# One fused attention and expert kernel: low parts of late weights on VectorE, low hidden products last, the last pair of heads two slots later

## The chip, the cores and the metric

The kernel runs on one core of one Trainium2 chip. The metric is the device time of one execution in microseconds. TensorE (PE in the profile) multiplies matrices, VectorE (DVE), ScalarE (ACT) and GpSimd (POOL) work elementwise, and SyncE (SP) and ScalarE issue the transfers. Each engine works through its own queue in order. "Idle" in a row is the time for which an engine stood still just before an instruction, with what ended it.

## The reference, cut to what matters

```python
# attention: 2 x 8 heads, 576 positions, head size 64
scores = scale * np.matmul(q, k.transpose(0, 1, 3, 2))
kth = np.partition(scores, -32, axis=-1)[..., -32:-31]
scores = np.where(scores >= kth, scores, -1e9)
attn = exp(scores - max); attn /= attn.sum(-1) + 1e-9
x = attn @ v                       # as 1152 tokens x 512
# part 1: 4 experts, 1024 hidden
p = domain_probs / domain_probs.sum(-1)
out = sum(p[:, e] * (np.maximum(x @ w1[e], 0) @ w2[e]) for e in range(4))
# part 2: 768 hidden, weights in float64
h = np.maximum(np.maximum(out @ m1, out @ m2), out @ m3)
return h @ mo
```

The weights of the first part are float32. Those of the second come as float64 and are converted on the chip.

## The kernel before, in words

The 1152 tokens are nine tiles of 128. Attention goes through 36 pairs (tile, two heads), eight slots each. `attention()` puts every step of a pair into a slot by a preset (`LOOSE`, `TIGHT` and so on, with the slots of `pv`, `turn`, `rec`, `last`), and yields once per slot.

Matrix products in float32 are made of three fast ones: each operand is split into a high part (rounded) and a low part (the rest). `product()`, lines 677 to 683, issues three matmuls: high times low, high times high, low times high. A weight of 128x1024 is loaded by SyncE, its high part `whi` is copied by ScalarE (L272), and its low part `wlo` is a subtraction on GpSimd (in two halves) or VectorE (whole), both at L278. `W_AHEAD` = 4 weights are split ahead of use. A weight's place in the list, counted from the first of stage 7, is `late`: below zero it goes to GpSimd, from there on by turns to GpSimd (even) and VectorE (odd).

Part 1 runs in stages over one to three tiles. Stage 0 is tile 0 alone and has its own code (`first_alone`). Stages 1 to 6 have two tiles, stage 7 has three (tiles 6, 7, 8) and stage 8 two (7, 8). Each stage does half of the experts' hidden blocks: for each i of four, `half1` for two units (first layer, ReLU on ScalarE, low part by a subtraction that reads PSUM on VectorE, L825, or, each fourth time, on GpSimd through a copy in SBUF, L816 to L818), and then `half2` of the i before (second layer, accumulated over an even and an odd i in one PSUM bank per tile). After an odd i the sum is scaled by the gate into `acc` (L742, L744).

`experts()` and the later stages are one generator of TensorE work. The main loop keeps two planned times, of TensorE and of VectorE, and after each slot lets out products until TensorE's planned time reaches the goal, which grows with VectorE's. Evacuations are queued by `later()`, and each `tick()` issues the next step of all that are queued.

From slot 306 on, one piece of the second part's weights per two slots goes through `to_float32`: two steps on ScalarE, three on VectorE (L242, L244, L246), an integer add on GpSimd (L249), and a store issued by ScalarE (L254) three slots later. Once attention has run out of slots, each slot adds `PAUSE` = 0.8 us to the goal.

Behind stage 8, `turned()` transposes three `acc` tiles into `x2`, high part on ScalarE (L907), low part `x2l` on VectorE (L908), for `largest()`, the second part. Its weights go by turns to GpSimd and VectorE too.

Of the kernel before, what the change touches and what calls it, by code (L numbers as in the profile page):

```python
# [10 lines left out]
F32 = mybir.dt.float32  # L11
# [49 lines left out]
def kernel(  # L61
# [41 lines left out]
    HALVES = [range(E) if not n % 2 else range(E, 2 * E) for n in range(len(STAGES))]  # L103
    WHOLE = [n for n, x in enumerate(STAGES) if len(x) == 1]
    FIRST_IN = {t: min(n for n, x in enumerate(STAGES) if t in x) for t in range(NTILE)}
# [93 lines left out]

    def whole(key):  # L200
        return key[1] in "ab" and key[0] in WHOLE

    def w_load_to(n):
        while w_pos["load"] < min(n, len(order)):
            key, src = order[w_pos["load"]]
            if key[1] in "cd" and narrowed[0] < WIDE * (narrow_at[key[2:]] + 1):
                return
            if whole(key):
                w_pos["load"] += 1
                continue  # L210
            raw = wp.tile([P, 1024], F32, tag="raw", bufs=5, name="raw")
            nc.sync.dma_start(out=raw, in_=src)
            w_raw[key] = raw
            w_pos["load"] += 1
# [42 lines left out]
    def w_split_to(n):  # L257
        while w_pos["split"] < min(n, len(order)):
            w_load_to(w_pos["split"] + 1)
            if w_pos["load"] == w_pos["split"]:  # L260
                return
            key, src = order[w_pos["split"]]
            if whole(key):
                w_hl[key] = wp.tile([P, 1024], F32, tag=("hi", "lo")[key[3]], name="whole")
                nc.sync.dma_start(out=w_hl[key], in_=src)
                w_pos["split"] += 1
                w_load_to(w_pos["split"] + 3)
                continue
            raw = w_raw.pop(key)
            hi = wp.tile([P, 1024], F32R, tag="hi", name="whi")  # L270
            lo = wp.tile([P, 1024], F32R, tag="lo", name="wlo")
            nc.scalar.activation(out=hi, in_=raw, func=AF.Copy)  # L272

            late = w_pos["split"] - w_index[LATE, "a", HALVES[LATE][0], 0]
            on = nc.vector if late >= 0 and late % 2 else nc.gpsimd

            for x in (slice(0, 512), slice(512, 1024)) if on is nc.gpsimd else (slice(0, 1024),):
                on.tensor_tensor(out=lo[:, x], in0=raw[:, x], in1=hi[:, x].bitcast(F32), op=ALU.subtract)  # L278
            f = 512 if key[1] in "bd" else 256
            w_hl[key] = (hi.rearrange("p (a f) -> p a f", f=f), lo.rearrange("p (a f) -> p a f", f=f))  # L280
            w_pos["split"] += 1
            w_load_to(w_pos["split"] + 3)

    def weight(key, oldest=None):

        w_split_to(w_index[oldest or key] + W_AHEAD + 2 * whole(key))
        return w_hl[key]
# [270 lines left out]
    def attention():  # L558
# [4 lines left out]

        def options(n):
            return TIGHT if n == HP - 1 else SECOND if n == 2 * HP - 1 else MIDDLE if n in (HP - 2, 2 * HP - 3, 2 * HP - 2) else FIRST if n < 2 * HP else THIRD if n == 3 * HP - 1 else BOTH if n in ON_ACT[1] else LOOSE

# [30 lines left out]
        for n, (c, hp, t) in enumerate(pairs):  # L597
# [25 lines left out]
            two(s0 + o.get("turn", o["rec"] + 2), pr.trans_r)  # L623
            end = max(o["pv"], o["rec"] + 2) + o["lag"]
            if "norm" in o:
# [164 lines left out]
    def experts():  # L790
        begin = {}

        def half1(c, i, u):
            tiles = STAGES[c]
            N = len(tiles) * P
            if c in WHOLE:
                ps = bank("ps1")
                w = weight((c, "a", i, u)).rearrange("p (a f) -> p a f", f=256)
                for f in range(2):
                    for a in range(KT):  # L800
                        pe(4 * P)
                        nc.tensor.matmul(ps[:, f * P:(f + 1) * P], lhsT=w[:, a, f * P:(f + 1) * P], rhs=xfull[:, a, :], start=f == a == 0, stop=f == 1 and a == KT - 1)
                    yield True
                h = hp_.tile([P, 2, 512], F32, tag="h", bufs=4, name="hfull")[:, 0, 0:2 * P]
                later(lambda: [nc.scalar.activation(out=h, in_=ps[:, 0:2 * P], func=AF.Relu), made.add(("h", c, i, u))])
                yield h
                return
            for groups in layer1(weight((c, "a", i, u)), xs_of(tiles), N, begin.pop((c, i, u), None)):
# [4 lines left out]
            count = made_h[0] = made_h[0] + 1  # L813
            if ON_POOL_H and not count % ON_POOL_H:
                raw = ms.tile([P, 2 * WIDTH], F32, tag="tm", bufs=2, name="raw")
# [15 lines left out]

        def half2(c, i, hs, ti):
            t = STAGES[c][ti]
            if not i % 2:
                outs[t] = po.tile([P, DM], F32, tag="o", name="ps2") if ti < 2 else bank("ps2")
            ps = outs[t]
            assert {("h", c, i, 0), ("h", c, i, 1)} <= made
            if c in WHOLE:
                for u in range(2):
                    w = weight((c, "b", i, u), (c, "b", i, 0)).rearrange("p (f n) -> p f n", f=2)  # L840
                    for f in range(2):
                        pe(4 * DM)
                        nc.tensor.matmul(ps, lhsT=hs[u][:, f * P:(f + 1) * P], rhs=w[:, f, :], start=not i % 2 and u == f == 0, stop=i % 2 == 1 and u == f == 1)
                        yield True
            else:
                yield from layer2(ps, [weight((c, "b", i, u), (c, "b", i, 0)) for u in range(2)], hs, len(STAGES[c]) * P, ti, not i % 2, i % 2 == 1)
            if not i % 2:
                return
            first = t not in accs
            if first:  # L850
                sums(t)
            later(*[lambda: None] * E_LAG, gated(ps, t, i // 2, first, c == LAST_IN[t] and i == HALVES[c][-1]))

        before = None
        for c in range(1, len(STAGES)):
# [14 lines left out]
            for i in HALVES[c]:  # L870
                hs = []
                for u in range(2):
                    for y in half1(c, i, u):
                        if y is not True:
                            hs.append(y)
                        yield True
                if i == HALVES[c][-1]:
                    x_free.update(t for t in STAGES[c] if LAST_IN[t] == c)
                if before is not None:
                    for ti in range(len(STAGES[before[0]])):  # L880
                        yield from half2(*before, ti)
                before = c, i, hs
        flush()
        yield from turned_ahead(len(STAGES))
        for ti in range(len(STAGES[before[0]])):
            yield from half2(*before, ti)
        flush()
# [193 lines left out]
```

## Time and profile before

| | |
|---|---|
| median of 3 runs | 752.12 us (752.11 to 752.51) |
| profiled execution, time | 752.02 us |
| profiled execution, span | 750.2 us |
| TensorE busy with matmuls | 721.8 us, 96% |
| mean granted TensorE clock | 0.997 |

The span runs from the first to the last instruction. The time of the profiled execution holds 1.8 us more than its span. A matmul's busy time overlaps the next one's, so the starts of two successive matmuls tell the rate.

### The profile page before, as it was taken

The page shows a single profiled execution, that of the slowest core. Times are in us where ns is not written, and L with a number is a line of the kernel's source. Part 1 is how long each engine was busy: PE and PEld are TensorE (multiplying, and loading weights), DVE is VectorE, ACT ScalarE, POOL GpSimd, SP SyncE. Part 2 cuts the span into 40 slices and gives each one's busy share as a digit, 9 for nine tenths or more (in the row PEclk, how much of TensorE's full clock was granted, in tenths as well). Part 3 has the DMA queues.
Part 4 walks back from the last instruction along what each step waited for, and adds up shares of the span by engine and source line. Part 5 has one row for each costly group of instructions (what it writes and reads, how often), then busy time and mean ns, then how long its engine had stood idle before and what let it go on. Part 6 is the DMA issues. An engine that isn't in the chain of part 4 may idle for free. (4 is left out here: it accounts for less than half of the span.)

```text
span 750.2 us, 13770 instructions
## 1 busy us (share of the span) xinstructions
PE 721.8 (96%) x4758; PEld 642.7 (86%) x4758; DVE 579.1 (77%) x1161; ACT 508.0 (68%) x1137; POOL 495.2 (66%) x432
## 2 busy tenths in 40 slices
PE   6799999999999999999999998999999899999998
PEld 3576788888989989898989977899989799999996
DVE  6999989989999899999999964887778544233341
ACT  4668889899978787788788856576656633433531
POOL 2514778679979797697778659888768743442520
PEclk9999999999999999999999999999999999999999
DMA  7584565535647364445444355889979742453501
GB/s 221 179 267 158 154 183 159 154 127 159 192 123 212 110 189 124 149 134 166 134 132 153 114 183 168 298 297 301 297 239 314 257 149 82 151 172 99 195 4 42
DMA packets 56487, 130.16 MB, mean 173 GB/s; under 512 B 9761, under 2 KB 23329, under 8 KB 56417
## 3 DMA queue, kind: packets, MB, share of 16 engines
q1 hardware_dynamic: 48064, 120.69, 51.5%
q10 hardware_dynamic: 8352, 8.59, 3.2%
q8 instruction: 37, 0.61, 0.3%
q14 instruction: 34, 0.27, 0.1%
HBM read 120.60 MB, written 8.65 MB: 172 GB/s over the span
## 5 line engine op out<-in xcount | busy, mean ns | idle before, releaser
L278 POOL TENSOR_TENSOR wlo<-raw,whi 128x512 fp32r<-128x512 f32 x258 | 340.4, 1348 | 119.4 <-ACT whi L272 115.9
L272 ACT ACTIVATE whi<-raw 128x1024 fp32r<-128x1024 f32 x164 | 169.7, 1056 | 36.2 <-PE ps L683 12.9
L681 PE MATMUL ps<-xl,whi 128*128 128x256 f32 (+1 forms) x584 | 173.7, 297 | 0.4 <-POOL xl L556 0.4
L683 PE MATMUL ps<-xh,wlo 128*128 128x256 f32 (+1 forms) x584 | 170.8, 292 | 0.0
L682 PE MATMUL ps<-xh,whi 128*128 128x256 f32 (+1 forms) x584 | 170.7, 292 | 0.0
L444 DVE MAX8 m<-work 128x8 f32<-128x576 f32 x216 | 155.2, 745 | 0.1
L681 PEld LDWEIGHTS ps<-xl,whi 128*128 128x128 f32 x584 | 110.8, 190 | 1.7 <-POOL xl L556 0.6
L682 PEld LDWEIGHTS ps<-xh,whi 128*128 128x128 f32 x584 | 109.7, 188 | 0.8 <-issue 0.2
L683 PEld LDWEIGHTS ps<-xh,wlo 128*128 128x128 f32 x584 | 109.8, 188 | 0.0
L278 DVE TENSOR_TENSOR wlo<-raw,whi 128x1024 fp32r<-128x1024 f32 x35 | 56.2, 1606 | 66.3 <-ACT whi L272 48.9
L446 DVE MATCH_REPLACE8 work<-m,work 128x576 f32<-128x576 f32 x144 | 106.7, 742 | 0.0
L681 PE MATMUL ps<-wlo,h 128*128 128x512 f32 x224 | 91.1, 406 | 0.9 <-POOL wlo L278 0.9
L683 PE MATMUL ps<-whi,h 128*128 128x512 f32 x224 | 87.9, 393 | 3.5 <-POOL h L818 3.5
L682 PE MATMUL ps<-whi,h 128*128 128x512 f32 x224 | 87.8, 392 | 0.0
L431 ACT ACTIVATE s<-pss 128x288 f32<-128x288 f32 x144 | 51.2, 399 | 11.6 <-PE pss L419 11.1
L444 DVE MAX8 m<-s 128x8 f32<-128x576 f32 x72 | 53.8, 748 | 5.0 <-ACT s L431 5.0
L249 POOL TENSOR_TENSOR narrow<-narrow,raw 128x256 int32<-128x256 int32 x48 | 44.2, 927 | 17.1 <-DVE narrow L246 4.4
L683 PEld LDWEIGHTS ps<-whi,h 128*128 128x128 f32 x224 | 42.1, 188 | 13.9 <-POOL h L818 4.4
L446 DVE MATCH_REPLACE8 work<-m,s 128x576 f32<-128x576 f32 x72 | 53.4, 742 | 0.0
L681 PE MATMUL ps<-x2l,whi 128*128 128x384 f32 x144 | 49.1, 341 | 2.1 <-DVE x2l L908 2.1
L681 PEld LDWEIGHTS ps<-wlo,h 128*128 128x128 f32 x224 | 42.9, 192 | 9.1 <-POOL wlo L278 2.7
L683 PE MATMUL ps<-x2h,wlo 128*128 128x384 f32 x144 | 49.0, 341 | 0.0
(113 smaller groups left out, 1472.3 us busy)
## 6 DMA issues: line engine op xcount, KB each, us to landing
raw<-in_w_dram SPq DMA_DIRECT2D x128, 512.0 KB, 4.2
raw<-narrow SPq DMA_DIRECT2D x36, 512.0 KB, 4.0
raw<-in_m_dram SPq DMA_DIRECT2D x36, 256.0 KB, 4.7
whole<-in_w_dram SPq DMA_DIRECT2D x14, 512.0 KB, 5.4
narrow<-narrow ACTq DMA_DIRECT2D x48, 128.0 KB, 4.8
kraw<-in_k_dram SPq DMA_DIRECT2D x16, 288.0 KB, 4.5
qraw<-in_q_dram SPq DMA_DIRECT2D x48, 64.0 KB, 3.9
raw<-in_mo_dram SPq DMA_DIRECT2D x12, 256.0 KB, 4.7
```

The lines of the kernel that those rows point to most:

```text
L249: nc.gpsimd.tensor_tensor(out=out.bitcast(I32), in0=out.bitcast(I32), in1=last, op=ALU.add)
L272: nc.scalar.activation(out=hi, in_=raw, func=AF.Copy)
L278: on.tensor_tensor(out=lo[:, x], in0=raw[:, x], in1=hi[:, x].bitcast(F32), op=ALU.subtract)
L431: nc.scalar.activation(out=s[:, h, :], in_=halves[h][:, 0:SH], func=AF.Copy)
L444: nc.vector.max(m[:, 8 * r:8 * r + 8], src)
L446: nc.vector.match_replace(out=self.w[j], in_to_replace=m[:, 8 * r:8 * r + 8], in_values=src, imm_value=NEG)
L681: nc.tensor.matmul(ps, lhsT=lh, rhs=rl, start=first, stop=False)
L682: nc.tensor.matmul(ps, lhsT=lh, rhs=rh, start=False, stop=False)
L683: nc.tensor.matmul(ps, lhsT=ll, rhs=rh, start=False, stop=last)
```

## The change

The diff removes `whole` and the branches on `WHOLE` (not shown in full), sends all first-part weights from `late` = 0 on to VectorE, keeps GpSimd out of the hidden low parts from stage 7 on, issues the products with low hidden parts after all the others in `half2`, and gives the last pair of heads a preset of its own.

```diff
@@ w_split_to
-            on = nc.vector if late >= 0 and late % 2 else nc.gpsimd
+            on = nc.vector if late >= 0 and (key[1] in "ab" or late % 2) else nc.gpsimd
@@ weight
-        w_split_to(w_index[oldest or key] + W_AHEAD + 2 * whole(key))
+        w_split_to(w_index[oldest or key] + W_AHEAD)
@@ attention
         def options(n):
+            if n == NTILE * HP - 1:
+                return dict(LOOSE, pv=19, turn=19, last=25)
...
-            end = max(o["pv"], o["rec"] + 2) + o["lag"]
+            end = max(o["pv"], o.get("turn", o["rec"] + 2)) + o["lag"]
@@ half1
-            if ON_POOL_H and not count % ON_POOL_H:
+            if ON_POOL_H and not count % ON_POOL_H and c < LATE:
@@ half2
-        def half2(c, i, hs, ti):
-            t = STAGES[c][ti]
+        def half2(c, i, hs):
+            tiles = STAGES[c]
+            N = len(tiles) * P
+            assert {("h", c, i, 0), ("h", c, i, 1)} <= made
             if not i % 2:
-                outs[t] = po.tile([P, DM], F32, tag="o", name="ps2") if ti < 2 else bank("ps2")
...
-                yield from layer2(ps, [weight((c, "b", i, u), (c, "b", i, 0)) for u in range(2)], hs, len(STAGES[c]) * P, ti, not i % 2, i % 2 == 1)
...
+                for ti, t in enumerate(tiles):
+                    outs[t] = po.tile([P, DM], F32, tag="o", name="ps2") if ti < 2 else bank("ps2")
+            for ti, t in enumerate(tiles):
                 for u in range(2):
...
+                    whi, wlo = weight((c, "b", i, u), (c, "b", i, 0))
                     for f in range(2):
...
+                        hi = hs[u][0][:, f * N + ti * P:f * N + (ti + 1) * P]
+                        pe(2 * DM)
+                        nc.tensor.matmul(outs[t], lhsT=hi, rhs=wlo[:, f, :], start=not i % 2 and u == f == 0, stop=False)
+                        nc.tensor.matmul(outs[t], lhsT=hi, rhs=whi[:, f, :], start=False, stop=False)
+                    yield True
+            for ti, t in enumerate(tiles):
+                for u in range(2):
+                    whi, _ = weight((c, "b", i, u), (c, "b", i, 0))
+                    for f in range(2):
+                        pe(DM)
+                        nc.tensor.matmul(outs[t], lhsT=hs[u][1][:, f * N + ti * P:f * N + (ti + 1) * P], rhs=whi[:, f, :], start=False, stop=i % 2 == 1 and u == f == 1)
+                yield True
+                if i % 2:
+                    first = t not in accs
+                    if first:
+                        sums(t)
+                    later(*[lambda: None] * E_LAG, gated(outs[t], t, i // 2, first, c == LAST_IN[t] and i == HALVES[c][-1]))
```

## Rows read from the trace of the kernel before

**Rows 1.** The page's busy table: busy us, share of the span, instructions.
```profile
PE 721.8 (96%) x4758; PEld 642.7 (86%) x4758; DVE 579.1 (77%) x1161; ACT 508.0 (68%) x1137; POOL 495.2 (66%) x432
```
**Rows 2.** What TensorE waited for, whole span: us in total, times, longest.
```profile
PE psv L532 <- ACT pt L498: 5.3, 6, 1.5
...
PE ps L683 <- POOL h L818: 3.5, 2, 2.2
PE ps L681 <- DVE x2l L908: 2.1, 1, 2.1
...
PE ps L681 <- POOL wlo L278: 0.9, 3, 0.3
```
**Rows 3.** Busy time by stretch: PE, PEld, DVE, ACT, POOL, granted clock, DMA share, GB/s.
```profile
470.00:592.00 122.00, 120.65 (x673) 108.68 (x671) 94.50 (x168) 80.14 (x154) 97.47 (x82) 1.00 0.86 285
592.00:596.00 4.00, 3.29 (x10) 3.32 (x11) 3.97 (x8) 1.48 (x3) 4.00 (x4) 0.59 0.97 349
```
**Rows 4.** TensorE in order of time: start, us, instruction, idle before it.
```profile
158.62 0.50 PE L683 MATMUL ps<-whi,h 128*128 128x512 f32 x1 [1.30 <-POOL h L818]
...
452.68 0.40 PE L681 MATMUL ps<-wlo,h 128*128 128x512 f32 x1
...
454.31 0.39 PE L682 MATMUL ps<-whi,h 128*128 128x512 f32 x1
456.93 0.50 PE L683 MATMUL ps<-whi,h 128*128 128x512 f32 x1 [2.24 <-POOL h L818]
...
592.71 0.65 PE L681 MATMUL ps<-x2l,whi 128*128 128x384 f32 x1 [2.06 <-DVE x2l L908]
```
**Rows 5.** GpSimd in order of time, before TensorE's wait at 454 us.
```profile
449.90 5.06 POOL L278 TENSOR_TENSOR wlo<-raw,whi 128x512 fp32r<-128x512 f32 x4 [1.12 <-ACT whi L272]
454.93 0.73 POOL L249 TENSOR_TENSOR narrow<-narrow,raw 128x256 int32<-128x256 int32 x1
455.62 1.26 POOL L818 TENSOR_TENSOR h<-raw,h 128x512 fp32r<-128x512 f32 x1
```
**Rows 6.** Groups of instructions by shape, 470 to 592 us: busy, mean ns | idle.
```profile
L278 POOL TENSOR_TENSOR wlo<-raw,whi 128x512 fp32r<-128x512 f32 x37 | 54.2, 1486 | 6.2 <-ACT whi L272 4.2 <-DMA narrow<-narrow 1.4 <-DMA raw<-in_m_dram 0.5
...
L249 POOL TENSOR_TENSOR narrow<-narrow,raw 128x256 int32<-128x256 int32 x40 | 37.4, 941 | 14.4 <-DVE narrow L246 4.4 <-DMA raw<-in_w_dram 4.0 <-DMA raw<-in_m_dram 2.4
L278 DVE TENSOR_TENSOR wlo<-raw,whi 128x1024 fp32r<-128x1024 f32 x18 | 31.0, 1724 | 20.2 <-ACT whi L272 13.8 <-DMA narrow<-narrow 3.2 <-issue 3.0
...
L825 DVE SCALAR_TENSOR_TENSOR hl<-ps,hh 128x384 fp32r<-128x384 f32 x12 | 6.2, 552 | 0.9 <-ACT hh L823 0.8
...
L825 DVE SCALAR_TENSOR_TENSOR h<-ps,h 128x512 fp32r<-128x512 f32 x6 | 4.1, 688 | 0.5 <-ACT h L823 0.4
L818 POOL TENSOR_TENSOR h<-raw,h 128x512 fp32r<-128x512 f32 x3 | 3.9, 1298 | 1.1 <-DMA raw<-in_mo_dram 1.1
L818 POOL TENSOR_TENSOR hl<-raw,hh 128x768 fp32r<-128x768 f32 x2 | 3.7, 1850 | 2.7 <-DMA raw<-in_w_dram 2.7
```
**Rows 7.** TensorE in order of time at the last pair of heads.
```profile
442.81 1.04 PE L490 MATMUL psp<-ident,p 128*128 128x128 f32 x8
...
445.41 0.49 PE L532 MATMUL psv<-pt,v_last 128*128 128x128 f32 x2 [1.45 <-ACT pt L498]
...
446.94 0.37 PE L681 MATMUL ps<-xl,whi 128*128 128x256 f32 x1
```
**Rows 8.** VectorE in order of time at the end of stage 8.
```profile
585.02 0.76 DVE L908 TENSOR_TENSOR x2l<-pst,x2h 128x384 fp32r<-128x384 f32 x2 [2.43 <-ACT x2h L907]
587.51 1.42 DVE L278 TENSOR_TENSOR wlo<-raw,whi 128x1024 fp32r<-128x1024 f32 x1 [1.74 <-issue]
...
590.10 0.75 DVE L908 TENSOR_TENSOR x2l<-pst,x2h 128x384 fp32r<-128x384 f32 x2
...
592.02 0.75 DVE L908 TENSOR_TENSOR x2l<-pst,x2h 128x384 fp32r<-128x384 f32 x2
```
**Rows 9.** VectorE's weight subtractions, 440 to 600 us: shortest, median, longest in ns.
```profile
L278 DVE TENSOR_TENSOR wlo<-raw,whi x19: 1218/1459/3869, 470.2 to 594.0; 128x1024 fp32r<-128x1024 f32 x19
```

More of the change, by code (lines that the diff above doesn't have):

```diff
@@ L103 @@
     HALVES = [range(E) if not n % 2 else range(E, 2 * E) for n in range(len(STAGES))]
-    WHOLE = [n for n, x in enumerate(STAGES) if len(x) == 1]
     FIRST_IN = {t: min(n for n, x in enumerate(STAGES) if t in x) for t in range(NTILE)}
@@ L198 @@
     w_pos = {"load": 0, "split": 0}
-    def whole(key):
-        return key[1] in "ab" and key[0] in WHOLE
     def w_load_to(n):
@@ L207, in w_load_to @@
                 return
-            if whole(key):
-                w_pos["load"] += 1
-                continue
             raw = wp.tile([P, 1024], F32, tag="raw", bufs=5, name="raw")
@@ L262, in w_split_to @@
             key, src = order[w_pos["split"]]
[L263 to L268, printed above, removed]
             raw = w_raw.pop(key)
@@ L795, in half1 @@
             N = len(tiles) * P
[L796 to L807, printed above, removed]
             for groups in layer1(weight((c, "a", i, u)), xs_of(tiles), N, begin.pop((c, i, u), None)):
@@ L830, in experts @@
         outs = {}
-        def half2(c, i, hs, ti):
-            t = STAGES[c][ti]
+        def half2(c, i, hs):
+            tiles = STAGES[c]
+            N = len(tiles) * P
+            assert {("h", c, i, 0), ("h", c, i, 1)} <= made
             if not i % 2:
-                outs[t] = po.tile([P, DM], F32, tag="o", name="ps2") if ti < 2 else bank("ps2")
-            ps = outs[t]
-            assert {("h", c, i, 0), ("h", c, i, 1)} <= made
-            if c in WHOLE:
+                for ti, t in enumerate(tiles):
+                    outs[t] = po.tile([P, DM], F32, tag="o", name="ps2") if ti < 2 else bank("ps2")
+            for ti, t in enumerate(tiles):
@@ L839, in half2 @@
                 for u in range(2):
-                    w = weight((c, "b", i, u), (c, "b", i, 0)).rearrange("p (f n) -> p f n", f=2)
+                    whi, wlo = weight((c, "b", i, u), (c, "b", i, 0))
                     for f in range(2):
[L842 to L845, printed above, removed]
-                yield from layer2(ps, [weight((c, "b", i, u), (c, "b", i, 0)) for u in range(2)], hs, len(STAGES[c]) * P, ti, not i % 2, i % 2 == 1)
@@ L847, in half2 @@
[L847 to L852, printed above, removed]
+                        hi = hs[u][0][:, f * N + ti * P:f * N + (ti + 1) * P]
+                        pe(2 * DM)
+                        nc.tensor.matmul(outs[t], lhsT=hi, rhs=wlo[:, f, :], start=not i % 2 and u == f == 0, stop=False)
+                        nc.tensor.matmul(outs[t], lhsT=hi, rhs=whi[:, f, :], start=False, stop=False)
@@ L879, in experts @@
                 if before is not None:
-                    for ti in range(len(STAGES[before[0]])):
-                        yield from half2(*before, ti)
+                    yield from half2(*before)
                 before = c, i, hs
@@ L884, in experts @@
         yield from turned_ahead(len(STAGES))
-        for ti in range(len(STAGES[before[0]])):
-            yield from half2(*before, ti)
+        yield from half2(*before)
         flush()
```

## The prediction

> **What bounds the kernel now.** I read the busy table first: TensorE's matmuls cover 96% of the span, VectorE 77%, GpSimd 66% [rows 1]. So a time can come only out of the 28.4 us in which TensorE does nothing, or be added to them. The second view was what TensorE waited for [rows 2]. Two kinds of its waits lie at places that the diff touches: low parts of a hidden layer that GpSimd computed (3.5 us, two waits), and the low part of the second layer's input, `x2l` (2.1 us, one wait). The wait for `pt` by the heads' output (5.3 us, six waits) is touched in the last pair alone. Waits for `wlo`, the low weights, are 0.9 us in all: weights are not late now.
>
> The third view splits the end by stretch [rows 3]. From 470 to 592 us (stages 7 and 8 with the conversion of the second part's weights) TensorE is busy 120.65 of 122 us, VectorE 94.50, GpSimd 97.47. So this stretch is TensorE's, and making GpSimd lighter in it gives nothing by itself. Right behind it, from 592 to 596 us, the granted clock is 0.59 of 2.4 GHz, that is, mostly the lower of its two levels (1.2 GHz), after 2.06 us in which TensorE stood still [rows 3, 4]. That stop costs 2.06 + 4 x 0.41 = 3.7 us.
>
> **Dead code.** `WHOLE` holds only stage 0, and `experts()` and the weight list start at stage 1. No instruction goes with `whole` and its branches: 0.
>
> **Low products last.** The number of matmuls and their shapes stay the same; only the order changes, so TensorE's work is unchanged. What moves is when the low part of `h` is needed. At 452.68 a second-layer block of stage 6 begins; its eighth matmul starts at 454.31 (0.23 us each), and the ninth, the first to read the second unit's low part, starts at 456.93 after 2.24 us [rows 4]. GpSimd is why: it took up four half subtractions at 449.90 (5.06 us) and the low part only at 455.62, for 1.26 us [rows 5]. In the new order 16 matmuls with high parts and two low ones of the first unit come before it: 18 x 0.23 = 4.1 us, so it is wanted at 456.8, and it is there at 456.9. The wait falls to about 0.1, if GpSimd's order stays. It may not: the late slots (below) put up to one more conversion add (0.94 us, rows 6) in front. Bounds of the gain 1.2 to 2.24; I take 1.8. The other wait of this kind, 1.30 us at 158.62 [rows 4], is covered in the same way. But there attention is still running, and TensorE's next products can find the heads' data not ready; bounds 0 to 1.30, I take half, 0.7.
>
> The order has a price. In a block that closes a tile, the tick that issues the waiting ReLU sat after the first tile's 12 matmuls, and now sits after 20: 8 x 0.23 = 1.8 us later, with only four matmuls before the subtraction is issued on VectorE. There are 12 such blocks in stages 1 to 6. VectorE may stand still in front of that subtraction; behind it are the top-k instructions. Bound from below 0, from above one subtraction (0.69 us, rows 6) each, 8 us. I take 0: the ReLU's input is by then long complete, so only ScalarE's own queue can hold it, and TensorE feels it only where its lead is gone. In stage 7 the second unit's subtraction comes after 32 matmuls and not 24, so two PSUM banks are held 1.8 us longer, in two blocks: 0 to 3.7 us, taken as 0, since the next block of products wants them only after this one has ended.
>
> **VectorE takes the late low weights.** 34 first-part weights stand from the index `late` = 0 on (16 of stage 7, 16 of stage 8, the last two of stage 6). 17 go to VectorE now, 34 after. The 17 that leave GpSimd are 34 halves of 1.486 us, 50.5 us; the four hidden low parts that leave it (two of 1.85, two of 1.30) are 6.3 us [rows 6]. ScalarE loses four copies. On VectorE the four cost 4 x 0.552 + 2 x 0.688 = 3.6 us (two PSUM banks each in stage 7). The weights are the open price: in this stretch 18 subtractions cost 31.0 us, mean 1.724 [rows 6], but single ones run from 1.218 to 3.869 with a median of 1.459 [rows 9]. With mean m for the 35 that there will be, VectorE has 94.5 - 31.0 + 3.6 + 35m of 122 us:
> m = 1.218 gives 109.7 (90%); m = 1.459 gives 118.2 (97%); m = 1.724 gives 127.4, 5.4 us too much. The point is m = 1.57. I take the median, because the long ones are those that met a GpSimd subtraction, most of which go.
>
> The Trainium skill, "SBUF — State Buffer", Who interferes with whom, says that a VectorE instruction with two SBUF inputs and a GpSimd one that reads SBUF take turns at one shared port, each blocked for the other's whole length. By that rule, what is left to collide with is the conversion's add, and m would be near the shortest, 1.218, so VectorE 90% busy. The trace agrees as far as a spread of 1.218 to 3.869 us for one shape can show it.
>
> So at 97% TensorE need not wait, but the cover is thin. Queued behind these subtractions on VectorE are the hidden low parts (wanted 16 matmuls later than now), the gated sums, which free the output banks, and the conversion's three steps. I cost it at 0, with 0 to 5.4 as bounds.
>
> **The end of stage 8.** TensorE waits for the third tile's `x2l`. VectorE's order there: `x2l` of the first tile at 585.02 after 2.43 us of idling, a weight at 587.51 after 1.74 more, a conversion, `x2l` at 590.10, a conversion, the last `x2l` at 592.02 [rows 8]. None of these is removed: this weight already belongs to the second part, whose alternation stays. The second `x2l` is issued later in the new order (behind the first tile's low products), the third where it was. So two conversions, one weight and two `x2l` remain between 587.5 and the end, and the 3.7 us stay. Up to 1.7 us of lag on VectorE is absorbed by its idling there. Bounds: the whole 3.7 gained, or 5.4 more lost (the excess above); taken 0.
>
> **The last pair.** Its transposes at 442.81 are followed, with no product in between, by a wait of 1.45 us and the `psv` products at 445.41; expert products return at 446.94 [rows 7]. Two more slots in between add nothing to the goal that lets products in: no top-k is left, only the reciprocal, 0.13 by the plan's own costs, while the nine transposes have put TensorE 0.97 ahead by them. So the 1.45 stays, and bounds are 0 and 1.45; taken 0. The conversion still starts at slot 306, but 2 of the 0.8 us pauses no longer lie before it, so it begins up to 1.6 us earlier beside the products; four more `dve()` entries (2.9 us) let products run ahead later. Neither is on TensorE's path. The changed `end` formula acts only in presets without `norm`, where it gives the old value except in the last pair.
>
> **Sum.** The profiled execution took 752.02 us (span 750.2), the median of runs is 752.12. 752.02 - 1.8 - 0.7 = 749.5; on the median's scale 749.6.
>
> **Rivals.**
> *Holes go at the end too.* A lighter GpSimd lets ScalarE's conversion stores and copies go on time, the last `x2l` comes in time, and TensorE does not stop: 749.6 - 3.7 = 745.9. For it: GpSimd is 80% busy there now. Against: the 5 us of VectorE's own instructions in front of the last `x2l` [rows 8].
> *Nothing arrives.* What is gained at 158 and 454 us is given back at 592, because the `x2l` chain is paced by VectorE and the conversion and not by TensorE: about 751.9. For it: one in-order engine decides there. Against: VectorE idles 2.43 us there on a copy that needs TensorE's transposes.
> *VectorE becomes the bound, on the other side.* Low weights stay at 1.72 us, VectorE needs 127.4 of 122 us, `wlo` or `x2l` comes late and TensorE stops: 749.6 + 5.4 = 755.0. It decides from m = 1.57 on. For it: the mean of now; against: the median.
>
> **How the numbers follow.** This kernel's runs lie within 0.4 us, so 0.2%, 1.5 us, is about what tells from no change. Chances: forecast 0.42, holes at the end 0.14, nothing arrives 0.22, VectorE bound 0.22. Faster holds the first two, 0.56; same 0.22; slower 0.22. The likeliest time is 749.6, its own range 748 to 750.6. The range reaches to both outer cases, 745.2 to 755.2.
>
> **What would show it.** No TensorE wait of over 0.5 us for a hidden low part; VectorE's weight subtractions of 470 to 592 us at 1.3 to 1.5 us; VectorE over 90% busy there; the stop before the second part's first product still about 2 us, with the slow clock behind it; 1.4 us before the last `psv`. The forecast is wrong if TensorE gets new waits for `wlo` or for PSUM in stages 7 and 8, if the last `x2l` shifts by more than a microsecond either way, or if the finer yields (6 for 4 in a block of two tiles) reshuffle attention's waits by more than the 2.5 us at stake.

## The result, and the profile after

The changed kernel takes 758.64 us (median of four, 757.98 to 759.38) against 752.15 for the kernel before beside it: a ratio of 1.0085, 95% interval 1.0068 to 1.0103. The forecast was 749.6, so the sign was wrong and the range (to 755.2) missed the time. The profiled execution took 759.38 us, its span is 757.5: 7.3 us more than before.

The busy table of the changed kernel, as in [rows 1]:

```profile
PE 727.1 (96%) x4758; PEld 642.5 (85%) x4758; DVE 599.2 (79%) x1184; ACT 505.5 (67%) x1133; POOL 442.5 (58%) x394
```

GpSimd lost 53 us and VectorE took on 20, as meant. TensorE has the same 4758 matmuls, and yet is "busy" 5.3 us longer: small stalls hide in that number, as a block below shows. What TensorE waited for in the changed kernel, whole span (as in [rows 2]):

```profile
PE psv L519 <- ACT pt L485: 5.9, 9, 1.5
...
PE ps L822 <- POOL wlo L265: 3.9, 9, 0.5
PE ps L670 <- DVE narrow L239: 1.6, 2, 1.2
...
PE psp L477 <- DVE p L459: 1.0, 1, 1.0
PE ps L670 <- DVE x2l L890: 0.7, 1, 0.7
```

The 3.5 us of waits for hidden low parts are gone, and the wait for `x2l` fell from 2.1 to 0.7. But the low weights `wlo` rose from 0.9 us (three waits) to 3.9 (nine), a wait for the heads' `p` of 1.0 is new, and so is 1.6 for `narrow`, VectorE's conversion step, which stands in the queue ahead of what TensorE needs.

Where the time went is read from events that both traces hold: the start of the last `psv` products, of stage 7, of the transposes behind stage 8, of the second part, and of the last matmul.

| event | before, us | after, us | later by |
|---|---|---|---|
| last `psv` products | 445.41 | 450.42 | 5.0 |
| stage 7 | 472.64 | 480.26 | 7.6 |
| first `pst` transposes | 583.69 | 593.48 | 9.8 |
| second part | 592.71 | 601.17 | 8.5 |
| last matmul | 746.26 | 753.20 | 6.9 |

So 5.0 us are lost while attention still runs, 4.8 up to the end of stage 8, and 2.9 come back. The first loss is read from VectorE. Busy time by stretch of the changed kernel, columns as in [rows 3]:

```profile
60.00:447.00 387.00, 378.46 (x2819) 330.08 (x2817) 361.94 (x771) 318.81 (x768) 301.23 (x266) 1.00 0.49 149
451.00:455.00 4.00, 4.00 (x26) 3.37 (x27) 0.69 (x2) 1.31 (x5) 0.47 (x1) 0.60 0.26 104
480.00:601.00 121.00, 118.77 (x662) 106.84 (x660) 104.76 (x185) 75.41 (x144) 44.06 (x42) 1.00 0.82 272
601.00:605.00 4.00, 3.83 (x22) 3.84 (x23) 4.00 (x6) 2.33 (x5) 2.80 (x3) 1.00 0.95 318
```

The same view of the kernel before, for the same work as the first of these lines:

```profile
60.00:442.00 382.00, 374.82 (x2817) 330.18 (x2816) 362.07 (x771) 318.71 (x768) 301.94 (x266) 1.00 0.50 151
```

VectorE does the same 771 instructions in the same 362 us, 94 to 95% of the stretch, and the stretch is 5 us longer. TensorE is shown busy for 98% of it, but this includes short stops: at the median distance from start to start of each of its shapes, its matmuls there would need about 342 us in either kernel (an estimate from the two traces). VectorE has only 20 us to spare, so it is the tighter of the two, and where it stands still counts. What it waits for there, the largest row of the kernel before and then of the changed one (total, times, longest):

```profile
DVE h L825 <- ACT h L823: 12.8, 12, 3.5
```
```profile
DVE h L802 <- ACT h L800: 17.3, 14, 3.5
```

That is 4.5 us more: the subtraction for `h` waits for its ReLU. Followed instruction by instruction, though, these are not 4.5 of the 5.0. VectorE's delay against the kernel before grows by 0.4 us at 109 us (a longer wait for scores), by 1.0 at 128, 0.5 at 207, 0.5 at 310 and 0.6 from 361 to 374, all four at places where the wait for `h` grew, and by 2.0 at 395. There no `h` is waited for. A mask behind the top-k takes 3.08 us and not 1.11, while GpSimd works through three subtractions (first the mask and GpSimd in the changed kernel, then the mask in the kernel before):

```profile
395.61 3.08 DVE L459 SCALAR_TENSOR_TENSOR p<-s,m,p 128x576 f32<-128x576 f32 x1
394.84 2.54 POOL L265 TENSOR_TENSOR wlo<-raw,whi 128x512 fp32r<-128x512 f32 x2
397.33 0.75 POOL L355 TENSOR_TENSOR ql<-qraw,qh 128x256 fp32r<-128x256 f32 x1
```
```profile
392.61 1.11 DVE L472 SCALAR_TENSOR_TENSOR p<-s,m,p 128x576 f32<-128x576 f32 x1
```

So about half of the 5.0 us comes at the waits for `h`; most of the rest of their 4.5 us is made up by masks just ahead of three of them, each about 0.7 us shorter than before. One of the places, on VectorE in order of time, changed kernel:

```profile
372.23 0.09 DVE L459 DVE_READ_ACCUMULATOR p<-s,m,p 128x1 f32 x1
373.75 0.69 DVE L802 SCALAR_TENSOR_TENSOR h<-ps,h 128x512 fp32r<-128x512 f32 x1 [1.44 <-ACT h L800]
374.36 0.75 DVE L431 MAX8 m<-s 128x8 f32<-128x576 f32 x1
```

ScalarE beside it:

```profile
366.21 0.61 ACT L800 ACTIVATE h<-ps 128x512 fp32r<-128x512 f32 x1
...
369.14 1.99 ACT L259 ACTIVATE whi<-raw 128x1024 fp32r<-128x1024 f32 x2
...
371.44 0.68 ACT L418 ACTIVATE s<-pss 128x288 f32<-128x288 f32 x2
372.02 0.27 ACT L507 ACTIVATE r<-psr 128x128 f32<-128x128 f32 x1
372.18 1.06 ACT L259 ACTIVATE whi<-raw 128x1024 fp32r<-128x1024 f32 x1
373.13 0.59 ACT L800 ACTIVATE h<-ps 128x512 fp32r<-128x512 f32 x1
```

ScalarE does not idle from 366.21 to the end of this ReLU. VectorE came to the subtraction at 372.3 and stood until 373.75 with the top-k behind it. The same place in the kernel before, VectorE and then ScalarE:

```profile
368.96 1.57 DVE L472 SCALAR_TENSOR_TENSOR p<-s,m,p 128x576 f32<-128x576 f32 x1
370.76 0.69 DVE L825 SCALAR_TENSOR_TENSOR h<-ps,h 128x512 fp32r<-128x512 f32 x1 [0.22 <-ACT h L823]
```
```profile
363.70 2.02 ACT L272 ACTIVATE whi<-raw 128x1024 fp32r<-128x1024 f32 x2
...
369.18 1.07 ACT L272 ACTIVATE whi<-raw 128x1024 fp32r<-128x1024 f32 x1
370.13 0.60 ACT L823 ACTIVATE h<-ps 128x512 fp32r<-128x512 f32 x1
```

The ReLU stands behind a weight copy in both. The difference lies further ahead in ScalarE's queue: the block that closes a tile (the closing block) has its own ReLU now at 366.21 (359.00 before), and two weight copies that were done at 363.70 come at 369.14. So the ReLU that is waited for ends 3.0 us later, and VectorE is ready for it only 1.8 us later, since it was 2.5 us late and its mask took 0.81 us and not 1.57. The subtraction that waits is the first one behind the closing block, not the one whose ReLU the late tick issues (at 367.53, without a wait). The ReLU's input was there (the last of its unit's 24 matmuls starts at 371.36, the ReLU at 373.13); the order of ScalarE's queue held it.

The second loss, TensorE in order of time (as in [rows 4] and [rows 7]):

```profile
448.20 0.63 PE L477 MATMUL psp<-ident,p 128*128 128x128 f32 x4 [0.96 <-DVE p L459]
...
450.42 0.49 PE L519 MATMUL psv<-pt,v_last 128*128 128x128 f32 x2 [1.49 <-ACT pt L485]
...
472.30 0.50 PE L822 MATMUL ps<-wlo,h 128*128 128x512 f32 x1 [0.34 <-POOL wlo L265]
472.64 0.40 PE L823 MATMUL ps<-whi,h 128*128 128x512 f32 x1
473.54 0.51 PE L822 MATMUL ps<-wlo,h 128*128 128x512 f32 x1 [0.51 <-POOL wlo L265]
...
476.59 0.40 PE L822 MATMUL ps<-wlo,h 128*128 128x512 f32 x1
476.82 0.40 PE L823 MATMUL ps<-whi,h 128*128 128x512 f32 x1
...
478.44 1.98 PE L830 MATMUL ps<-whi,h 128*128 128x512 f32 x8
480.26 0.34 PE L670 MATMUL ps<-xl,whi 128*128 128x384 f32 x1
```

The stops of 0.96 and 1.49 us are followed by a granted clock of 0.60 from 451 to 455 us, which costs 4 x 0.40 = 1.6. The block from 472.30 to 480.26 has 24 matmuls, which at the 0.23 us that 476.59 to 476.82 shows would take 5.5; it takes 8.0, paced by GpSimd's halves, after a stop of 0.34. Against that stands the 2.24 of the wait that is gone [rows 4]: 1.6 + 2.5 + 0.3 - 2.2 = 2.2 of the 2.6 us between the last `psv` and stage 7. The idle notes there (0.34, 0.51 and two more of 0.50) add up to 1.85, not to 2.8, since a matmul after a stop is shown busy for 0.50. The next 2.2, in stages 7 and 8, are mostly the 1.64 for `narrow`. The way back is the stop before the second part (2.06 to 0.74, so 1.3) and the clock behind it (0.95 for 0.59 over 4 us, so 1.4).

### The profile page after: what moved, and what is told of

Read it like the earlier page. It is cut to its first block, busy times and chain, and to the rows that moved or that the text cites. A ratio compares the mean times of both kernels' runs of the same rounds, so it can differ in the third digit from the quotient of the medians.

```text
span 757.5 us, 13769 instructions
## 1 busy us (share of the span) xinstructions
PE 727.1 (96%) x4758; PEld 642.5 (85%) x4758; DVE 599.2 (79%) x1184; ACT 505.5 (67%) x1133; POOL 442.5 (58%) x394
## 5 line engine op out<-in xcount | busy, mean ns | idle before, releaser
L265 POOL TENSOR_TENSOR wlo<-raw,whi 128x512 fp32r<-128x512 f32 x224 | 291.1, 1330 | 125.4 <-ACT whi L259 121.5
L265 DVE TENSOR_TENSOR wlo<-raw,whi 128x1024 fp32r<-128x1024 f32 x52 | 75.5, 1459 | 57.5 <-ACT whi L259 44.6
L242 POOL TENSOR_TENSOR narrow<-narrow,raw 128x256 int32<-128x256 int32 x48 | 47.2, 986 | 79.5 <-DVE narrow L239 33.9
L823 PE MATMUL ps<-whi,h 128*128 128x512 f32 x224 | 87.9, 392 | 0.0
L830 PE MATMUL ps<-whi,h 128*128 128x512 f32 x224 | 59.3, 398 | 0.0
L671 PE MATMUL ps<-x2h,whi 128*128 128x384 f32 x144 | 48.3, 335 | 0.0
```

The source lines that it names most:

```text
L242: nc.gpsimd.tensor_tensor(out=out.bitcast(I32), in0=out.bitcast(I32), in1=last, op=ALU.add)
L671: nc.tensor.matmul(ps, lhsT=lh, rhs=rh, start=False, stop=False)
L823: nc.tensor.matmul(outs[t], lhsT=hi, rhs=whi[:, f, :], start=False, stop=False)
L830: nc.tensor.matmul(outs[t], lhsT=hs[u][1][:, f * N + ti * P:f * N + (ti + 1) * P], rhs=whi[:, f, :], start=False, stop=i % 2 == 1 and u == ...
```

## The experiments

All were timed in five rounds against the kernel before. "Order" means the new `half2`. It brings three things at once, which a list of steps takes apart: the order of the matmuls, how often the generator yields (after 4 matmuls for 6), and where the two ticks of a closing block fall (after 20 and 24 of 24 matmuls for 12 and 24).

### One part at a time

**e1_order**, the kernel before with the new `half2` alone (its first line; the rest as in the change):

```diff
-        def half2(c, i, hs, ti):
+        def half2(c, i, hs):
```

> The kernel before with the new order of half2 alone (low hidden products last, its six yields for four); weights, hidden low parts and the last pair as before. Theory A (the order costs, by making VectorE wait for ScalarE in stages 1 to 6): 755.5 to 758.5 us, VectorE's waits for h in 60 to 447 us near 17 us against 12.8, no TensorE wait for a low hidden part. Theory B (VectorE's added load in stages 7 and 8 costs): 749 to 751 us, the two TensorE waits for low hidden parts gone. Theory C (the last pair's slots cost): as B.

**e2_no_order**, the changed kernel with the old `half2` (its first line, as an edit of the changed kernel):

```diff
-        def half2(c, i, hs):
+        def half2(c, i, hs, ti):
```

> The changed kernel with the old order of half2: VectorE has the late weights and hidden low parts, the last pair is in its later slots. Theory A: 749 to 753 us, VectorE's waits for h back at some 13 us, and the stop before the second part's first product stays short (under 1 us). Theory B: 756 to 760 us, with TensorE waits between 470 and 592 us. Theory C: 756 us or more, with the loss between 440 and 455 us.

**e3_last_pair**, the kernel before with the last pair's preset alone:

```diff
+            if n == NTILE * HP - 1:
+                return dict(LOOSE, pv=19, turn=19, last=25)
```

> The kernel before with the last pair's later slots alone. Theories A and B: 751.5 to 753 us. Theory C: 755 us or more. The wait of 1.45 us for the last psv stays in all of them.

**e4_vector**, the kernel before with weights and hidden low parts moved to VectorE:

```diff
-            on = nc.vector if late >= 0 and late % 2 else nc.gpsimd
+            on = nc.vector if late >= 0 and (key[1] in "ab" or late % 2) else nc.gpsimd
-            if ON_POOL_H and not count % ON_POOL_H:
+            if ON_POOL_H and not count % ON_POOL_H and c < LATE:
```

> The kernel before with the late low weights and the hidden low parts of stages 7 and 8 on VectorE, order and slots as before. Theory A: 748.5 to 752.5 us: the stop before the second part's first product falls from 2.06 to some 0.7 us and the slow clock behind it goes (3 us gained), up to 2 us of new TensorE waits in stage 7. Theory B: 755 us or more.

| | median us | ratio (95%) | VectorE's waits for `h` to 447 us | `wlo` waits | `x2l` stop |
|---|---|---|---|---|---|
| e1_order | 760.00 | 1.0118 (1.0097 to 1.0140) | 18.3 | 4.6 | 2.0 |
| e2_no_order | 751.78 | 1.0007 (0.9993 to 1.0020) | 12.8 | 0.8 | 0.7 |
| e3_last_pair | 751.95 | 1.0002 (0.9990 to 1.0015) | 12.8 | 0.8 | 1.4 |
| e4_vector | 754.04 | 1.0030 (1.0015 to 1.0044) | 12.8 | 0.6 | 2.7 |

As expected were e2_no_order and e3_last_pair. e1_order is slower than Theory A's range (760.00 for at most 758.5), with the waits that it named (18.3 for 17). e4_vector lies between its two ranges, and its stop did not fall as Theory A had it.

The whole loss comes with the new `half2`; without it the rest of the change is even. The last pair alone does nothing, as forecast. The VectorE part alone costs 0.3%, with the `x2l` stop at 2.7 us and not shorter; together with the last pair the stop is 0.7 and the cost is gone. The last pair's slots alone bring it to 1.4 and move no time. So the shorter stop needs those slots; a lighter GpSimd alone does not give it.

### What in the new `half2` costs

Each of the next four is the kernel before with a `half2` made from this list, where `LOW_LAST` is the new order and `T` the stage's tiles. The edits shown are against this `half2` with a yield after 4 and late ticks; n counts its matmuls:

```python
LOW_LAST = [(ti, u, f, k) for ti in T for u in range(2) for f in range(2) for k in "ab"] + [(ti, u, f, "c") for ti in T for u in range(2) for f in range(2)]
# a: wlo times high h, b: whi times high h, c: whi times low h
```

**e5_yields**: `LOW_LAST`, yields as of old, ticks late as in the change.

```diff
-                if n % 4 == 0:
+                if n % 6 == 0:
                     yield True
```

> The new order of half2 alone, but it yields after every six matmuls, as the old order does, not after four; the ticks stay late (after 20 and 24 of 24 matmuls). Theory A1 (the late tick costs: the ReLU is issued just ahead of the subtraction that waits for it): 757 to 760 us, VectorE's waits for h in 60 to 447 us stay near 18 us. Theory A2 (the finer yields cost, they shift the products against attention's slots): 750 to 753 us, waits for h back near 13 us. Theory A3 (the order of the matmuls costs by itself, by wanting the low weights sooner): 756 us or more.

**e6_ticks**: `LOW_LAST`, a yield after 4, ticks where they were.

```diff
+                if i % 2 and n % 12 == 0 and n < 12 * n_t:
+                    tick()
```

> The new order of half2 alone with its yields after four matmuls, but the ticks stand where they were, after 12 and 24 of 24 matmuls, so the waiting ReLU is issued as early as before. Theory A1: 750 to 753 us, waits for h near 13 us. Theory A2: 757 to 760 us, waits for h near 18 us. Theory A3: 756 us or more.

**e7_both**: `LOW_LAST` with both as of old, so the order of the matmuls alone.

> The new order of half2 alone with both yields and ticks where the old order has them: only the order of the matmuls differs from the kernel before. Theories A1 and A2: 749.5 to 752 us, the two waits for low hidden parts gone, waits for h near 13 us. Theory A3: 755 us or more, with TensorE waits for wlo of some 4 us.

**e8_high_first** (edit against e7_both): as e7_both, but all products high times high first, then those with `wlo`, then those with low `h`.

```diff
-            steps = LOW_LAST
+            steps = [(ti, u, f, k) for k in "bac" for ti in T for u in range(2) for f in range(2)]
```

> As the run with both yields and ticks of the old order, but all products of two high parts come first, then those with low weights, then those with low hidden parts. Theories A1 and A2: 748.5 to 751.5 us, 0 to 1 us under the run beside it, since the waits for wlo go too. Theory A3 (wanting low weights sooner costs): clearly under the run beside it, by 3 us or more.

| | order | yield after | ticks | median us | ratio (95%) | waits for `h` | `wlo` waits |
|---|---|---|---|---|---|---|---|
| e1_order | new | 4 | late | 760.00 | 1.0118 (1.0097 to 1.0140) | 18.3 | 4.6 |
| e5_yields | new | 6 | late | 755.42 | 1.0047 (1.0030 to 1.0064) | 15.5 | 3.8 |
| e6_ticks | new | 4 | as of old | 758.11 | 1.0086 (1.0071 to 1.0102) | 13.4 | 3.8 |
| e7_both | new | 6 | as of old | 752.92 | 1.0025 (1.0003 to 1.0048) | 13.0 | 3.6 |
| e8_high_first | high first | 6 | as of old | 751.18 | 0.9998 (0.9983 to 1.0012) | 12.9 | 1.5 |

None of the three theories fits alone: e5_yields hit none of the ranges, in time or in waits; e6_ticks has a time of Theories A2 and A3 and the waits of A1; e7_both lies between its ranges, with A3's waits for `wlo`; e8_high_first lies in the range of A1 and A2.

Two costs stand apart. The late tick: from e7_both to e5_yields, run together, the median grows by 2.5 us and VectorE's waits for `h` by the same 2.5. That the two are equal is luck: by the ratios it is 0.22% (1.7 us), and the two intervals overlap, so this pair alone does not settle it. The fine yields: from e7_both to e6_ticks 5.2 us, with VectorE's waits nearly unchanged. With late ticks they cost as much (4.6 us by the medians, e5_yields to e1_order), and there the waits for `h` grow too, by 2.8. The order that is left costs 0.25%, of which 0.10% is one execution of the twelve (761.13 us; without it the ratio is 1.0015). In the changed kernel it is 0.25% as well (e2_no_order to e12_all_both, below). Its low-hidden waits (3.5 us) are gone, but `wlo` went up by 2.7 and the wait of `psv` for `pt` by 0.7 (6.0 for 5.3). TensorE's waits for `wlo` in e7_both, and in e8_high_first (total, times, longest):

```profile
PE ps L845 <- POOL wlo L278: 3.6, 8, 0.5
```
```profile
PE ps L845 <- POOL wlo L278: 1.5, 2, 0.7
```

Putting the eight high times high products ahead of the first `wlo` takes back 2.1 us of waits, and the time is level with before. In the changed kernel the same step takes back 0.29% (e12_all_both to e11_high_first_all, below).

### Why fine yields cost, and whether anything wins

**e9_old_fine** (edit against e6_ticks): old order of matmuls, a yield after 4.

```diff
-            steps = LOW_LAST
+            steps = [(ti, u, f, k) for ti in T for u in range(2) for f in range(2) for k in "abc"]
```

> The kernel before with its old order of matmuls and its ticks, but half2 yields after every four matmuls, not six: nothing else differs. If finer yields cost by themselves (theory A2): 754.5 to 757.5 us. If they cost only together with the new order: 751 to 753 us.

**e10_lead**: as e6_ticks, with TensorE let 0.43 us further ahead in the plan. The idea was that a finer yield overshoots the goal by less, so that TensorE's lead is smaller.

```diff
-        while clock["pe"] < clock["goal"]:
+        while clock["pe"] < clock["goal"] + 0.43:
```

> The new order with yields after four matmuls and the old ticks (758.1 us before), and products are let out until the planned time of TensorE is 0.43 us past the goal, which is what six matmuls overshoot more than four at most. If finer yields cost because TensorE's products then come with less lead over the attention steps: 752 to 755 us, and no TensorE wait for the last pair's mask before its transposes. If they cost by where the products happen to fall: 757 to 760 us, or any other shift of over 2 us with other waits.

**e11_high_first_all**: e8_high_first with the VectorE part and the last pair's preset.

> Candidate for the best: high products first, then low weights, then low hidden parts, with the old yields and ticks, and with VectorE's late weights and hidden low parts and the last pair's later slots. If the parts add up (0.9998 and 1.0007): 750 to 753 us. If VectorE's share helps once the order is repaired, as it took 0.3% off the new order: 747 to 750 us.

**e12_all_both**: the changed kernel with yields after 6 and ticks as of old.

> The changed kernel with two repairs: half2 yields after six matmuls and ticks after 12 and 24, as the old order does. If yields and ticks explain the loss: 751 to 754 us, against 758.6. If VectorE's load in stages 7 and 8 holds part of it: 755 us or more.

**e13_old_late**: old order, a yield after 6, ticks after 20 and 24, so the late tick alone.

> The kernel before with its old order of matmuls and its yields after six; only the ticks of a closing block come after 20 and 24 of 24 matmuls, not after 12 and 24, as in the new order. VectorE and ScalarE then have the same queues as in the run with the new order and yields after six. If the late tick costs by itself (A1): 753.5 to 756 us, VectorE's waits for h in 60 to 447 us near 15.5. If it costs only together with the new order of matmuls: 751 to 753 us.

**e14_all_ticks**: the changed kernel with the ticks as of old, yields after 4.

> The changed kernel with its ticks moved back to 12 and 24, yields still after four. If the late tick is most of the loss: 752.5 to 755.5 us. If the finer yields hold as much: 755.5 to 758 us.

**e15_all_yields**: the changed kernel with yields after 6, ticks late.

> The changed kernel with yields after six matmuls, ticks still late. If the finer yields are most of the loss: 753 to 755 us. If the late tick holds as much: 755 to 758 us.

| | median us | ratio (95%) | waits for `h` | `wlo` waits |
|---|---|---|---|---|
| e9_old_fine | 752.50 | 1.0003 (0.9989 to 1.0017) | 13.2 | 0.8 |
| e10_lead | 762.62 | 1.0144 (1.0124 to 1.0165) | 15.7 | 5.2 |
| e11_high_first_all | 752.12 | 1.0003 (0.9991 to 1.0015) | 12.9 | 1.8 |
| e12_all_both | 753.61 | 1.0032 (1.0019 to 1.0046) | 13.0 | 4.1 |
| e13_old_late | 753.55 | 1.0019 (1.0000 to 1.0038) | 15.2 | 0.6 |
| e14_all_ticks | 756.48 | 1.0057 (1.0037 to 1.0076) | 13.5 | 3.3 |
| e15_all_yields | 756.52 | 1.0056 (1.0036 to 1.0075) | 16.5 | 4.4 |

All seven came out in one of their ranges: e9_old_fine in that of a cost that comes only with the new order, e11_high_first_all in that of parts that add up, e12_all_both in that of yields and ticks, e13_old_late at the edge of the late tick's, e14_all_ticks and e15_all_yields in that of two equal costs, and e10_lead in its last, a shift of over 2 us with other waits.

*The late tick* makes VectorE wait. Leaving e10_lead aside (ticks as of old and 15.7 us, at other places), the kernels with late ticks wait 15.2 to 18.3 us for `h` and all others 12.8 to 13.5, whatever their order and yields. Alone on the old order it adds 2.4 us:

```profile
DVE h L825 <- ACT h L823: 15.2, 13, 3.5
```

Nearly all that is added lies at five subtractions. The wait at each, in us (0: none noted):

| starts in the changed kernel at | before | e13: late tick | e9: fine yields | e7: new order | e5: new, late | e6: new, fine | e1: new, both | changed |
|---|---|---|---|---|---|---|---|---|
| 128.27 | 0 | 0.24 | 0 | 0 | 0.29 | 0 | 1.46 | 0.65 |
| 207.44 | 0 | 0 | 0 | 0 | 0 | 0.46 | 0.36 | 0.44 |
| 310.26 | 0.23 | 0.24 | 0.22 | 0.23 | 0.22 | 0.30 | 1.44 | 1.44 |
| 373.75 | 0.22 | 1.47 | 0.21 | 0.30 | 1.44 | 0.30 | 1.44 | 1.44 |
| 437.51 | 0.34 | 1.14 | 0.59 | 0 | 1.14 | 0 | 1.14 | 1.13 |

The late tick alone brings the waits at 373.75 and 437.51; the one at 310.26 needs fine yields and the new order as well. Only the first row is a subtraction whose own ReLU the late tick issues. The other four are the first behind a closing block, as in the rows at 372 us. In time, the five pairs that differ by the late tick alone all point one way: 0.19% (to e13_old_late), 0.22 (e7_both to e5_yields), 0.32 (e6_ticks to e1_order), 0.24 (e12_all_both to e15_all_yields) and 0.28 (e14_all_ticks to the change), so 1.4 to 2.4 us. Some of the single intervals touch zero (that of e13_old_late does).

*The lead* is not borne out: with more of it the kernel was slower than e6_ticks by 4.5 us, and the wait for `p` stayed.

*The fine yields* cost nothing on the old order (1.0003) and 5.2 us on the new (e7_both to e6_ticks). The wait for `p` before the last transposes comes with them every time, here in e9_old_fine:

```profile
PE psp L490 <- DVE p L472: 1.0, 1, 1.0
```

As it is there at no cost in e9_old_fine, it is not by itself the price. In e6_ticks it is followed by more. TensorE's waits in order of time, then the busy time by stretch:

```profile
445.32 0.63 PE L490 MATMUL psp<-ident,p 128*128 128x128 f32 x4 [0.96 <-DVE p L472]
447.55 0.49 PE L532 MATMUL psv<-pt,v_last 128*128 128x128 f32 x2 [1.49 <-ACT pt L498]
468.46 0.50 PE L845 MATMUL ps<-wlo,h 128*128 128x512 f32 x1 [1.25 <-POOL wlo L278]
469.71 0.50 PE L845 MATMUL ps<-wlo,h 128*128 128x512 f32 x1 [0.51 <-POOL wlo L278]
470.95 0.79 PE L845 MATMUL ps<-wlo,h 128*128 128x512 f32 x1 [0.51 <-POOL wlo L278]
```
```profile
468.00:475.00 7.00, 5.49 (x13) 3.33 (x14) 4.58 (x8) 5.02 (x10) 7.00 (x6) 0.67 0.98 331
475.00:480.00 5.00, 5.00 (x21) 4.21 (x20) 1.35 (x4) 2.50 (x4) 4.08 (x6) 0.78 0.73 249
```

TensorE meets a `wlo` that is 1.25 us late, and the granted clock is 0.67 and 0.78 in the 12 us behind: 7 x 0.33 + 5 x 0.22 = 3.4 us. The other 1.9 of the 5.2 are there before: by that much VectorE is later than in e7_both at the end of attention. In the changed kernel the fine yields cost 0.25% (e12_all_both to e14_all_ticks) to 0.29% (e15_all_yields to the change). In the first of these pairs it is the clock again: in the profile of e14_all_ticks it is 0.58 over 447 to 451 us and 0.93 over 455 to 480, 3.4 us in all, in that of e12_all_both 1.00 in both. In the second pair, the profile of the change has the clock of 0.60 at 451 to 455 (1.6 us) and the mask of 3.08 us, which in e15_all_yields takes 1.10; there the clock is 1.00.

Over all executions the clock says the same. With the mean clock c of an execution, the mean of (1 - c) x span is 6.3 us in e6_ticks for 1.6 in e7_both, 4.7 in e1_order for 2.4 in e5_yields, 2.5 in e14_all_ticks for 0.8 in e12_all_both, and 1.9 in the changed kernel for 0.8 in e15_all_yields. On the old order the fine yields do not raise it: 1.5 in e9_old_fine, 3.3 in the kernel before beside it. So on the new order the fine yields come with lost clock, and with late ticks with waits for `h` on top. Which of the new stops lower the clock, and why finer yields bring them on the new order alone, stays open. The late tick, in contrast, is not a matter of the clock: over its four pairs on the new order this quantity moves by 0.8, -1.6, 0.1 and -0.6 us.

*No version wins.* e11_high_first_all, with all that proved harmless, is level with the kernel before.

## Why the prediction was wrong, point by point

**"Low products last": the order has a price, "I take 0".** This is the step that failed. It named the mechanism, a VectorE standing still in front of the subtraction for `h`, with bounds 0 to 8 us, and took 0 because the ReLU's input is long complete. It added that only ScalarE's own queue could hold the ReLU, and did not price that; this is what happened. VectorE's waits for `h` grew by 4.5 us in the changed kernel. About 2.6 us of the 5.0 by which attention ends later lie at these places, 2.0 at the mask of 3.08 us, and no term of the sum had that either. The waits are also not where the prediction looked: four of the five subtractions concerned come behind the closing block. The runs price the late tick at 1.4 to 2.4 us. The prediction judged the cover by TensorE's lead; the row that decides is VectorE's busy share to 447 us, which was not read.

**The finer yields** had no term in the sum. They stood in the last sentence alone, as something that would make the forecast wrong if it moved attention's waits by more than 2.5 us; it was 5.0 with the late tick. They cost about as much as the tick in the changed kernel, 0.29% (to e15_all_yields), and more without the rest of the change.

**"Weights are not late now."** True of the kernel before (0.9 us), and carried over to an order that it does not describe. In the old order a half of `wlo` feeds three matmuls before the next half is wanted, in the new two. GpSimd makes a half in 1.25 us (472.30 to 473.54 in the rows after), more than two or three products of 0.23 last, so where it paces the block the new order has one product less under each wait. The order alone costs 0.25% (e7_both), and putting high times high first takes it back (e8_high_first).

**The gains of 1.8 and 0.7.** The waits for hidden low parts went, as forecast, and nothing arrived: e7_both has 3.5 us of them less and 3.4 us more of `wlo` and `pt`. The rival "nothing arrives" had the right kind of outcome from another cause. The prediction also took 0.4 us for the spread of the times, from three of them; 29 executions of the kernel before beside the first experiments go from 749.65 to 754.66, so a gain of 2.5 us could not have been told by a few.

**VectorE takes the weights.** Cost 0 was right with the last pair's slots (e2_no_order, 1.0007), but the size behind it was not: m was forecast at 1.459, 97% busy. The subtractions of 440 to 601 us in the changed kernel, by shortest, median and longest in ns, as in [rows 9]:

```profile
L265 DVE TENSOR_TENSOR wlo<-raw,whi x35: 1215/1218/5499, 472.2 to 597.3; 128x1024 fp32r<-128x1024 f32 x35
```

The median is the shortest length, and VectorE is 104.76 of 121 us busy, 87%. The one of 5.5 us starts at 472.2, beside the last four GpSimd halves. By a rule of the Trainium skill's "SBUF — State Buffer", Who interferes with whom, the prediction had worked out 1.218 and 90% as a rival; the trace agrees with it. The rival "VectorE becomes the bound" did not happen in stages 7 and 8; what is seen there of the price is TensorE's new wait for VectorE's `narrow`, 1.6 us.

**The end of stage 8.** "The 3.7 us stay" was wrong in the changed kernel: the stop is 0.74 us, and the clock behind it 0.95. The rival "holes go at the end too" had this effect, though not by its reason alone: with the lighter GpSimd and without the last pair's slots the stop is 2.7 us (e4_vector). It was worth 2.7 us there, and was outweighed.

**The last pair.** The 1.45 us stay (1.49), as forecast, and its preset alone is 1.0002.

**The sum by the runs**, in the changed kernel: all but `half2` 0.07% (e2_no_order), the order 0.25% (to e12_all_both), and from there the late tick 0.24% (to e15_all_yields) and the fine yields 0.25% (to e14_all_ticks): 0.81% against 0.85% measured. Each of these differences is uncertain by some 0.2% either way, and the parts do not act independently (e1_order is slower than the whole change; the mask of 3.08 us takes 1.1 in all other profiles but e10_lead's, 2.03), so the split is rough. That the loss as a whole belongs to the new `half2` is shown by e2_no_order (1.0007).

## What to carry to other kernels

Before a wait on the busiest engine is traded away, ask which engine sets the length of that stretch: here VectorE, 95% busy, which ended attention 5 us later while TensorE's waits for hidden low parts went. A change of loop order in a generator also changes where evacuations are issued and how finely work is interleaved; keep these fixed and price them one by one. And operands that another engine makes just in time are wanted in a certain order: begin with the products that need none of them.

## What the runs showed of the hardware that was not expected

The half-speed stretch moved from edit to edit, and some profiles have none. Before, it is at 592 to 596 us with a granted clock of 0.59, behind a stop of 2.06 us [rows 3, 4]. After, it is at 451 to 455 with 0.60, behind stops of 0.96 and 1.49 us within 4 us in which TensorE was busy for 1.55:

```profile
447.00:451.00 4.00, 1.55 (x12) 0.99 (x11) 1.20 (x4) 2.20 (x8) 0.46 (x1) 0.98 0.83 229
```

Four stops of 0.34 to 0.51 us between 472 and 476 were not followed by a fall (1.00 from 455 to 480 and on to 601). In e8_high_first's profiled execution the mean clock is 1.000. The quantity (1 - c) x span is 0 to 3.8 us in executions of one and the same e5_yields. Not all of it is lost time: fitted over all experiments, each execution against the mean of its own kernel, the time moves by 0.66 us for one us of it. That is still as much as most of the parts tried here are worth, and a reason to look at the clock before a difference of 2 us is explained by a wait.

A VectorE instruction with two SBUF inputs can take several times its usual length beside GpSimd: the mask took 3.08 us at 395.61 beside three GpSimd subtractions and 0.81 at 371.49, and VectorE's weight subtraction 5.50 us beside four GpSimd halves and 1.218 at the median. Which of them are hit changes with small shifts of the plan.
